# Squared-ReLU attention into a PReLU MLP: another order of the head, and bursts of three chunks, A@V and three chunks

## The chip, the cores and the metric

The kernel runs on one core of a Trainium2 chip. The metric is the device time of one execution, in microseconds (us). The core has a matrix engine (TensorE, PE in the profile, with its weight loads shown as PEld), a vector engine (VectorE, DVE), a scalar engine (ScalarE, ACT), GpSimd (POOL) and SyncE (SP). Here POOL does little but start the loads from memory, and SP starts the stores and the transposing transfers. Matrix products land in PSUM, which has 8 banks of 512 float32 per partition; only ACT and DVE bring them out again.

## The reference

```python
def _attn_ref(q, k, v):                       # 8 batches, 12 heads, 448 rows, 64 columns
    scale = 1.0 / np.sqrt(q.shape[-1])
    scores = scale * np.matmul(q, k.transpose(0, 1, 3, 2))
    attn = np.maximum(scores, 0.0) ** 2 / S
    return np.matmul(attn, v)

def _moe_ref(x, w_in, w_out, alpha):          # x: 3584 x 768, w_in: 768 x 2048, w_out: 2048 x 768
    h = x @ w_in
    g = np.maximum(h, 0.0) + alpha * np.minimum(h, 0.0)
    return g @ w_out
```

Between the two the heads are put side by side, so that x has one row of 12 * 64 values for each batch and row.

## The kernel before

**The units.** Four heads of one batch are a quad. A batch b has three, n = 3b to 3b + 2, so there are 24. The 448 rows of a head are cut into 7 sets of 64. A *chunk* (n, j) is the scores of the 64 keys of set j against all 448 queries, for the four heads of the quad. It goes through four lines:

- `score_mm` (L175): four matmuls on 64x64 parts of the array, into a pair of PSUM banks;
- `relu`: out of PSUM to bf16, 128x896, on ACT (L184) or on DVE (L186), as a letter A or D in the program says;
- `square`: times itself, on DVE (L194) or, for one chunk alone, on ACT (L192);
- `attnv(n)` ("A@V", L204): 28 matmuls, four for each of the quad's seven squared chunks in order, into a pair of banks. They give x transposed, which comes out scaled: for quad 0 in one ACT instruction of 128x896 (L212), for all others in two halves, one on ACT (L214) and one on DVE (L215).

For each batch F1 (`f1`, L238) makes 16 column blocks of h, called ff 0 to 15, each of 6 matmuls with km 0 to 5. km 0 and 1 read the first quad's x, 2 and 3 the second's, 4 and 5 the third's. `f1_out` brings each out by a ReLU of the negative on ACT (`neg`, L246) and one DVE instruction that forms g (L247), and then squares one waiting chunk, if there is one (`sq(1)`). For each pair of batches F2 (`f2`, L261) makes 7 x 2 tiles of the output with 16 matmuls each. ACT copies them out of PSUM (`osb`, L263) and SP stores them (L269).

**Turned rows.** q and k must be turned for the scores. Quads 0 to 5 are turned by the matrix engine (`turn_pe`: 28 transposes at L150, then copies out of PSUM on DVE at L153 or on ACT at L155). Quads from 6 on are turned by a transfer (`turn_dma`): DVE writes q and k into one tile in another order (`perm`, L161, two instructions), and SP starts a transposing transfer (L163). `prepare(n)` is `turn_dma(n)` and the loads of quad n + 2.

**What sets the order.** The order is written by hand: each engine gets its instructions in the order of the program text, and each waits in that order for what it needs. SP's transposes and stores and POOL's loads stand in their queues likewise. A PSUM bank is taken by `take_bank` (the one taken longest ago), a pair by `take_pair`; this too is settled in the order of the text, so a change of the order moves all later work to other banks. `hold` takes a bank and keeps it out of the choice until `take` is called for it. Tiles come from pools with fixed counts of buffers: 3 for the rows of q and of k, 7 for v, 2 for `perm`, 4 for the turned rows, 7 for relu results, 12 for squares, 4 for outputs. A tile waits until the one that had its buffer is done with.

**The head** is the program up to the first F2 tile: quads 0, 1 and 2 with little else to do beside them, then F1 of batch 0 with the chunks of quads 3 and 4 between its blocks. The four banks for ff 0 to 3 are kept early, km 0 to 3 of ff 0 and 1 run before A@V of quad 2, and km 0 to 3 of ff 2 and 3 behind it; then km 4 and 5 of all four.

**The body.** F1 of batch 1 follows, then for each batch two stretches. In the F1 stretch three chunks (`run(some(3))`) stand ahead of ff 6 and of ff 12. In the F2 stretch stand three bursts, one for each quad of the next batch; `burst(n)` is three chunks, `attnv(n)`, two chunks, and then the squares. Between two bursts there are two F2 tiles in even batches and three in odd ones. `some` deals out the chunks of quads 6 to 23 in order with the letters A, D, A. The last batch has no chunks left.

Of the kernel before, what the change touches and what calls it, by code (L numbers as in the profile page):

```python
# [12 lines left out]
ACTF = mybir.ActivationFunctionType  # L13
ALU = mybir.AluOpType

PP = 64
NJ = 7
# [3 lines left out]
def kernel(  # L21
# [10 lines left out]
    nc = tc.nc  # L32
    B, H, S, D = q.shape
# [3 lines left out]
    KM = d_model // 128  # L37
# [24 lines left out]
    psum = ps_pool.tile([128, 8, 512], F32)  # L62


    taken = [0] * 8
    clock = [0]

    def take(lo, n):
        clock[0] += 1
        for i in range(lo, lo + n):  # L70
            taken[i] = clock[0]

    def take_pair():
        lo = min((0, 2, 4, 6), key=lambda i: (max(taken[i], taken[i + 1]), i))
        take(lo, 2)
        return psum[:, lo:lo + 2]

    def hold():

        i = min(range(8), key=lambda i: (taken[i], i))  # L80
        taken[i] = 10**9
        return i

    def take_bank():
        i = min(range(8), key=lambda i: (taken[i], i))
        take(i, 1)
        return psum[:, i]
# [54 lines left out]
    def turn_pe(n, cuts=((0, NJ, "D"),), cuts_k=((0, NJ, "D"),)):  # L142
        t = T_pool.tile([128, 2, NJ, 128], BF16, tag="T", name="T")
        for i, name in enumerate("qk"):
            src = raw.pop((n, name))
            for lo, hi, eng in (cuts, cuts_k)[i]:
                ps = take_bank().bitcast(BF16)
                for j in range(lo, hi):
                    for s in range(2):
                        nc.tensor.transpose(ps[64 * s:64 * s + 64, 128 * j:128 * j + 128], src[:, s, j], ident)  # L150
                dst = t[:, i, lo:hi].rearrange("p j c -> p (j c)")
                if eng == "D":
                    nc.vector.tensor_copy(dst, ps[:, 128 * lo:128 * hi])  # L153
                else:
                    nc.scalar.copy(dst, ps[:, 128 * lo:128 * hi])  # L155
        T[n] = t

    def turn_dma(n):
        p = perm_pool.tile([128, 2, NJ, 2, D], BF16, tag="perm", name="perm")
        for i, name in enumerate("qk"):  # L160
            nc.vector.tensor_copy(p[:, i], raw.pop((n, name)).rearrange("p s j d -> p j s d"))  # L161
        t = T_pool.tile([128, 2, NJ, 128], BF16, tag="T", name="T")
        nc.sync.dma_start_transpose(out=t.rearrange("p a j c -> p (a j) c"),  # L163
                                    in_=p.rearrange("p a j s d -> p (a j s d)"))
        T[n] = t
# [20 lines left out]
            nc.vector.tensor_scalar(rl, ps[:, :, :S], 0.0, None, ALU.max)  # L186
        return rl

    def square(n, j, rl, eng="D"):
        a = at_pool.tile([128, 2, S], BF16, tag="at", name="at")  # L190
        if eng == "A":
            nc.scalar.activation(a, rl, ACTF.Square)  # L192
        else:
            nc.vector.tensor_tensor(a, rl, rl, ALU.mult)  # L194
        att[(n, j)] = a

    def attnv(n):
        ps = take_pair()
        vv = vraw.pop(n)
        for j in range(NJ):  # L200
            a = att.pop((n, j))
            for r in range(2):
                for s in range(2):
                    nc.tensor.matmul(ps[64 * s:64 * s + 64, r, :S],  # L204
                                     vv[64 * r:64 * r + 64, s, j, :],
                                     a[64 * r:64 * r + 64, s],
                                     start=(j == 0), stop=(j == NJ - 1))
        b, g = divmod(n, NG)
        if g == 0:
            xT[b] = xT_pool.tile([128, NG, 2, S], BF16, tag="xT", name="xT")  # L210
        if n == 0:
            nc.scalar.activation(xT[b][:, g], ps[:, :, :S], ACTF.Copy, scale=out_scale)  # L212
            return
        nc.scalar.activation(xT[b][:, g, 0], ps[:, 0, :S], ACTF.Copy, scale=out_scale)  # L214
        nc.vector.tensor_scalar(xT[b][:, g, 1], ps[:, 1, :S], out_scale, None, ALU.mult)  # L215

    late = []

    def sc(chunks):

        for n, j, eng in chunks:
            late.append((n, j, relu(score_mm(n, j), eng)))

    def sq(k=99):
        for g in late[:k]:
            square(*g)
        del late[:k]

    def run(chunks):
        sc(chunks)  # L230
        sq()


    gT = {}

    def f1_mm(ps, b, ff, ks):
        for km in ks:
            nc.tensor.matmul(ps, w_in_sb[:, km // 2, km % 2, bass.ts(ff, 128)],  # L238
                             xT[b][:, km // 2, km % 2, :],
                             start=(km == 0), stop=(km == KM - 1))  # L240

    def f1_out(ps, b, ff):
        if b // 2 not in gT:
            gT[b // 2] = g_pool.tile([128, KF, 2 * S], BF16, tag="g", name="gT")
        neg = neg_pool.tile([128, S], F32, tag="neg", name="neg")
        nc.scalar.activation(neg, ps, ACTF.Relu, scale=-1.0)  # L246
        nc.vector.scalar_tensor_tensor(gT[b // 2][:, ff, (b % 2) * S:(b % 2) * S + S],  # L247
                                       neg, beta_sb[:, ff:ff + 1], ps, ALU.mult, ALU.add)
        sq(1)
# [24 lines left out]
    def ch(n, lo, hi, p=pat):  # L274
        return [(n, j, p[j]) for j in range(lo, hi)]

    load_w_in(0)
    load_w_in(1)
    turn_pe(0, ((0, 4, "D"), (4, NJ, "D")), ((0, 2, "A"), (2, NJ, "D")))
    sc(ch(0, 0, 4))  # L280
    sq(3)
    load_qk(3)
# [15 lines left out]
    sc([(1, 4, "D"), (1, 5, "A"), (1, 6, "A")])  # L298
    sq(2)
    load_w_out(0)  # L300
    early = {}
    todo = []

    def some_early(count):
        for ff, km in todo[:count]:
            if ff not in early:
                early[ff] = hold()
            f1_mm(psum[:, early[ff], :S], 0, ff, (km,))
        del todo[:count]

    sc(ch(2, 0, 3, "AAA"))
    sq(3)
    attnv(1)
    load_qk(5)
    load_v(5)
    load_w_out(1)
    todo = [(ff, km) for ff in range(4) for km in range(4)]
    sc(ch(2, 3, 4, "AAAAAAA"))
    nc.vector.tensor_scalar(beta_sb, alpha_sb, -1.0, 1.0, ALU.mult, ALU.add)
    sq(2)  # L320
    sc(ch(2, 4, 7, "AAAAADA"))
    some_early(8)
    square(*late.pop(-2), "A")
    sq()
    attnv(2)
    some_early(8)
    for ff in range(4):
        f1_mm(psum[:, early[ff], :S], 0, ff, range(4, KM))
        f1_out(psum[:, early[ff], :S], 0, ff)
        take(early[ff], 1)  # L330


    def f1s(b, lo, hi):
        for ff in range(lo, hi):
            f1(b, ff)
# [6 lines left out]
    def prepare(n):  # L342
        if n < NQ:
            turn_dma(n)
        load(n + 2)

    turn_pe(3)
    load_qk(6)
    load_v(6)
    f1s(0, 4, 6)  # L350
    sc(ch(3, 0, 3))
    f1s(0, 6, 8)
    sc(ch(3, 3, 6))
    f1s(0, 8, 10)
    turn_pe(4)
# [27 lines left out]
    def some(k):  # L383
        lo = at_c[0]
        at_c[0] = min(lo + k, len(chunks))
        return [(n, j, e) for (n, j), e in zip(chunks[lo:at_c[0]], "ADA")]

    def burst(n):

        sc(some(3))  # L390
        attnv(n)
        sc(some(2))
        sq()

    early = []
    for ff in range(4):
        ps = take_bank()[:, :S]
# [4 lines left out]
    for ff in range(KF):  # L402
        if ff < 4:
            f1_mm(early[ff], 1, ff, range(4, KM))
            f1_out(early[ff], 1, ff)
        else:
            f1(1, ff)
        if ff in (1, 4, 7):
            turn_dma(6 + ff // 3)
        if ff == 11:  # L410
            load(9)
            load(10)
    f2(0, 3, 0)
    run(some(3))
    f2(0, 3, 1)
    f2(0, 0, 1)
    prepare(9)
    run(some(3))
    f2(0, 1, 1)
    run(some(3))  # L420
    f2(0, 2, 1)
    run(some(3))
    f2(0, 4, 0)
    burst(6)
    f2(0, 4, 1)
    f2(0, 5, 0)
    prepare(10)
    burst(7)
    f2(0, 5, 1)
    f2(0, 6, 0)  # L430
    burst(8)
    f2(0, 6, 1)

    for b in range(2, B):
        n0 = NG * (b + 1)
        last = b == B - 1
        sb = b // 2
        for ff in range(KF):
            if not last and ff in (6, 12):
                run(some(3))  # L440
            if not last and ff in (1, 9):
                prepare(n0 + 2 + ff // 8)
            f1(b, ff)
        if b % 2 == 0:
            units = [(sb, c, h) for c in range(3) for h in range(2)]
            at = {1: 0, 3: 1, 5: 2}
        else:
            units = [(sb, c, h) for c in range(3, 7) for h in range(2)]
            at = {1: 0, 4: 1, 7: 2}
        for i, u in enumerate(units):  # L450
            if i in at and not last:
                g = at[i]
                if g == 1:
                    prepare(n0 + 4)
                burst(n0 + g)
            if last and i == len(units) - 1:
                f2(*u, parts=((0, 256), (256, HALF)))
            else:
                f2(*u)
# [30 lines left out]
```

## Time and profile before

| What | Value |
|---|---|
| Median of three runs | 389.79 us (389.78 to 390.1) |
| The profiled execution | 389.79 us; its span, from the first to the last instruction, 388.0 us |
| PE busy | 378.4 us of the span, 98% |
| DVE, ACT, POOL busy | 266.2 us, 203.8 us, 63.3 us |
| Granted TensorE clock | 0.998 of full speed |

How to read the views. The *page* gives busy times for the whole span. The *table by stage* gives, for each stretch of the span, how long each engine was busy. The *timeline* lists instructions in order of time, like ones in a row put together: start, length, engine, line, operation, output and inputs, shapes, count, and in brackets how long the engine had been idle and what ended it. The *chain* is the work that ended last, followed back from the end: start, length, and what it was. In a row of like instructions each begins before the one ahead of it has ended, so the length of one is more than the step from start to start; both are used below and told apart.

### The profile page before, as it was taken

What the parts mean: (1) busy time and instruction counts of PE and PEld (TensorE: products, weight loads), DVE (VectorE), ACT (ScalarE), POOL (GpSimd) and SP (SyncE); (2) the same over time, 40 slices, a digit from 0 to 9 for tenths busy, and PEclk for the clock granted to TensorE, in tenths of its full rate; (3) what the DMA queues carried; (4) which work ended last, traced back from release to release, by engine and by line L of the source; (5) the groups of instructions that cost most, each with busy time, mean ns of one, the idle gap of its engine ahead of it and who ended that gap; (6) DMA issues with size and microseconds to landing.
All of it is one profiled execution on the core that took longest, in us unless ns stands there. A gap on an engine that the chain in (4) does not pass through costs nothing.

```text
span 388.0 us, 7917 instructions
## 1 busy us (share of the span) xinstructions
PE 378.4 (98%) x3228; PEld 210.6 (54%) x3228; DVE 266.2 (69%) x422; ACT 203.8 (53%) x329; POOL 63.3 (16%) x94
## 2 busy tenths in 40 slices
PE   7799999999999999999999999999999999999996
PEld 5444454555665456644555455654555545655564
DVE  4977965776868878789755897689754887626300
ACT  5977656445545665466444564546543475434311
POOL 7468211422022102022010220120000000000000
PEclk9999999999999999999999999999999999999999
DMA  9999999899593775787292872937024300120023
GB/s 180 188 203 204 204 214 209 133 173 180 119 151 75 119 127 78 134 131 112 54 170 57 138 114 47 169 56 143 24 62 100 78 0 23 42 61 2 13 70 82
DMA packets 71093, 43.06 MB, mean 111 GB/s; under 512 B 38160, under 2 KB 71056, under 8 KB 71056
## 3 DMA queue, kind: packets, MB, share of 16 engines
q0 software_dynamic: 26496, 22.35, 39.6%
q1 hardware_dynamic: 44128, 19.65, 23.6%
q10 hardware_dynamic: 432, 0.56, 0.4%
q8 instruction: 25, 0.41, 0.4%
q14 instruction: 12, 0.10, 0.1%
HBM read 45.62 MB, written 11.01 MB: 146 GB/s over the span
## 4 chain that ended last, share of the span: by engine, by line
PE 90%; DVE 5%; ACT 2%; DMA 1%; issue 1%; ACTq 0%
PE psum L261 38%; PE psum L238 35%; PE psum L204 8%; PE psum L175 8%; DVE at L194 2%; ACT rl L184 2%; DMA qfirst<-in_q_dram 1%; DVE gT L247 1%; PE psum L150 1%; DVE T L153 1%; DVE rl L186 1%; ACT neg L246 0%; ACT osb L263 0%; DVE qraw L133 0%; ACTq L269 0%
## 5 line engine op out<-in xcount | busy, mean ns | idle before, releaser
L261 PE MATMUL psum<-w_out_sb,gT 128*128 128x384 bf16 (+2 forms) x912 | 151.1, 323 | 0.1
L238 PE MATMUL psum<-xT,w_in_sb 128*128 128x448 bf16 x768 | 149.5, 353 | 0.4 <-ACT rl L184 0.4
L261 PEld LDWEIGHTS <-gT 128*128 128x128 bf16 x912 | 86.7, 98 | 63.1 <-issue 8.6
L238 PEld LDWEIGHTS <-w_in_sb 128*128 128x128 bf16 x768 | 73.7, 98 | 72.3 <-issue 5.5
L246 ACT ACTIVATE neg<-psum 128x448 f32<-128x448 f32 x128 | 69.2, 546 | 66.2 <-PE psum L238 62.4
L247 DVE SCALAR_TENSOR_TENSOR gT<-neg,beta_sb,psum 128x448 bf16<-128x448 f32 x128 | 83.1, 676 | 29.5 <-ACT neg L246 29.5
L184 ACT ACTIVATE rl<-psum 128x896 bf16<-128x896 f32 x115 | 99.7, 934 | 0.5 <-PE psum L175 0.5
L194 DVE TENSOR_TENSOR at<-rl 128x896 bf16<-128x896 bf16 x167 | 93.7, 617 | 2.1 <-ACT rl L184 2.0
L186 DVE TENSOR_SCALAR rl<-psum 128x896 bf16<-128x896 f32 x53 | 57.5, 1086 | 40.3 <-PE psum L175 40.2
L263 ACT COPY osb<-psum 128x384 f32<-128x384 f32 (+2 forms) x57 | 27.0, 474 | 105.8 <-PE psum L261 98.9
L175 PE MATMUL psum<-T 64*64 64x448 bf16 x672 | 45.9, 356 | 2.4 <-ACT rl L184 0.9
L97 POOL DMA_DIRECT2D qraw<-in_q_dram x23 | 16.5, 717 | 179.1 <-DVE perm L161 167.6
L204 PE MATMUL psum<-at,vraw 64*64 64x448 bf16 x672 | 37.2, 351 | 0.6 <-ACT rl L184 0.2
L204 PEld LDWEIGHTS <-vraw 64*64 64x64 bf16 x672 | 23.9, 106 | 11.4 <-issue 3.2
L175 PEld LDWEIGHTS <-T 64*64 64x64 bf16 x672 | 18.0, 105 | 22.1 <-issue 15.6
L215 DVE TENSOR_SCALAR xT<-psum 128x448 bf16<-128x448 f32 x23 | 14.4, 625 | 16.0 <-PE psum L204 11.6
L97 POOL DMA_DIRECT2D kraw<-in_k_dram x23 | 16.5, 719 | 7.8 <-PE psum L175 4.8
L104 POOL DMA_DIRECT2D vraw<-in_v_dram x24 | 17.3, 722 | 2.0 <-DMA w_in_sb<-in_moe_w_in_dram 0.9
L214 ACT ACTIVATE xT<-psum 128x448 bf16<-128x448 f32 x23 | 12.7, 553 | 4.3 <-PE psum L204 4.3
L161 DVE COPY perm<-qraw 128x896 bf16<-128x896 bf16 x18 | 11.0, 611 | 4.9 <-DMA T<-perm 2.6
L114 POOL DMA_DIRECT2D w_in_sb<-in_moe_w_in_dram x16 | 10.0, 628 | 7.5 <-DMA kraw<-in_k_dram 2.5
L161 DVE COPY perm<-kraw 128x896 bf16<-128x896 bf16 x18 | 10.9, 608 | 0.0
(21 smaller groups left out, 35.3 us busy)
## 6 DMA issues: line engine op xcount, KB each, us to landing
out_dram<-osb SPq DMA_DIRECT2D x110, 96.0 KB, 2.2
vraw<-in_v_dram POOLq DMA_DIRECT2D x24, 224.0 KB, 7.4
qraw<-in_q_dram POOLq DMA_DIRECT2D x23, 224.0 KB, 4.7
kraw<-in_k_dram POOLq DMA_DIRECT2D x23, 224.0 KB, 6.7
w_in_sb<-in_moe_w_in_dram POOLq DMA_DIRECT2D x16, 192.0 KB, 8.2
w_out_sb<-in_moe_w_out_dram POOLq DMA_DIRECT2D x2, 1536.0 KB, 18.5
qfirst<-in_q_dram SPq DMA_DIRECT2D x1, 448.0 KB, 4.3
kfirst<-in_k_dram ACTq DMA_DIRECT2D x1, 448.0 KB, 4.6
```

The costliest lines, as they stand in the source:

```text
L97: nc.gpsimd.dma_start(out=t.rearrange("p m j d -> p m (j d)"), in_=flat[:, 2 * g:2 * g + 2])
L161: nc.vector.tensor_copy(p[:, i], raw.pop((n, name)).rearrange("p s j d -> p j s d"))
L175: nc.tensor.matmul(ps[64 * c:64 * c + 64, r, :S], t[64 * r:64 * r + 64, 1, j, 64 * c:64 * c + 64], t[64 * r:64 * r + 64, 0, :, 64 * c:64 * ...
L184: nc.scalar.activation(rl, ps[:, :, :S], ACTF.Relu)
L186: nc.vector.tensor_scalar(rl, ps[:, :, :S], 0.0, None, ALU.max)
L194: nc.vector.tensor_tensor(a, rl, rl, ALU.mult)
L204: nc.tensor.matmul(ps[64 * s:64 * s + 64, r, :S], vv[64 * r:64 * r + 64, s, j, :], a[64 * r:64 * r + 64, s], start=(j == 0), stop=(j == NJ ...
L238: nc.tensor.matmul(ps, w_in_sb[:, km // 2, km % 2, bass.ts(ff, 128)], xT[b][:, km // 2, km % 2, :], start=(km == 0), stop=(km == KM - 1))
L246: nc.scalar.activation(neg, ps, ACTF.Relu, scale=-1.0)
L247: nc.vector.scalar_tensor_tensor(gT[b // 2][:, ff, (b % 2) * S:(b % 2) * S + S], neg, beta_sb[:, ff:ff + 1], ps, ALU.mult, ALU.add)
L261: nc.tensor.matmul(ps, gT[sb][:, ff, bass.ts(c, 128)], w_out_sb[:, hf, ff, lo:hi], start=(ff == 0), stop=(ff == KF - 1))
L263: nc.scalar.copy(o[:, lo:hi], ps)
```

## The change

Eight things change.

1. In `turn_pe(0)` the copy of the first two sets of k's columns moves from ACT to DVE.
2. `attnv(1)` gets its result out in one ACT instruction of 128x896, as `attnv(0)` does, in place of two halves on ACT and DVE.
3. Ahead of `attnv(1)` stand two chunks of quad 2 and two squares, in place of three and three; the third chunk comes behind it. Three squares then follow where two did.
4. The squared chunk (2, 5) moves from ACT to DVE; `square` loses its ACT form.
5. Ahead of `attnv(2)` km 0 to 3 of ff 0 and 1 still run, but ff 2 and 3 no longer begin behind it; km 4 and 5 of ff 0 follow it at once. `hold` goes. ff 2 runs whole ahead of `turn_pe(3)`, and the blocks around the chunks of quad 3 are cut at 3, 5 and 8 in place of 4, 6 and 8. The new condition for the tile of g makes it at the same place as before.
6. A burst is three chunks, A@V, three chunks. For this the run of three chunks behind `f2(0, 2, 1)` goes, and in each F1 stretch the two runs ahead of ff 6 and ff 12 become one ahead of ff 8.
7. `turn_dma` of quads 6, 7 and 8 stands behind ff 1, 5 and 9 of batch 1 in place of 1, 4 and 7, and the loads of quads 9 and 10 behind ff 13 in place of 11.
8. `prepare(9)` moves behind `f2(0, 4, 0)`, ahead of the first burst, and `prepare(10)` ahead of the third. In the later batches it stands at ff 8 and ahead of the first and third bursts, in place of ff 1, ff 9 and ahead of the second burst.

```diff
-    if eng == "A":
-        nc.scalar.activation(a, rl, ACTF.Square)
-    else:
-        nc.vector.tensor_tensor(a, rl, rl, ALU.mult)
+    nc.vector.tensor_tensor(a, rl, rl, ALU.mult)
...
-    if n == 0:
+    if n < 2:
         nc.scalar.activation(xT[b][:, g], ps[:, :, :S], ACTF.Copy, scale=out_scale)
         return
...
-    if b // 2 not in gT:
+    if b % 2 == 0 and ff == 0:
...
-turn_pe(0, ((0, 4, "D"), (4, NJ, "D")), ((0, 2, "A"), (2, NJ, "D")))
+turn_pe(0, ((0, 4, "D"), (4, NJ, "D")), ((0, 2, "D"), (2, NJ, "D")))
...
-sc(ch(2, 0, 3, "AAA"))
-sq(3)
+sc(ch(2, 0, 2, "AA"))
+sq(2)
 attnv(1)
 ...
-todo = [(ff, km) for ff in range(4) for km in range(4)]
-sc(ch(2, 3, 4, "AAAAAAA"))
+sc(ch(2, 2, 4, "AAAAAAA"))
 nc.vector.tensor_scalar(beta_sb, alpha_sb, -1.0, 1.0, ALU.mult, ALU.add)
-sq(2)
+sq(3)
 sc(ch(2, 4, 7, "AAAAADA"))
-some_early(8)
-square(*late.pop(-2), "A")
 sq()
+early = []
+for ff in range(2):
+    ps = take_bank()[:, :S]
+    f1_mm(ps, 0, ff, range(4))
+    early.append(ps)
 attnv(2)
-some_early(8)
-for ff in range(4):
-    f1_mm(psum[:, early[ff], :S], 0, ff, range(4, KM))
-    f1_out(psum[:, early[ff], :S], 0, ff)
-    take(early[ff], 1)
+for ff in range(2):
+    f1_mm(early[ff], 0, ff, range(4, KM))
+    f1_out(early[ff], 0, ff)
...
+f1s(0, 2, 3)
 turn_pe(3)
 load_qk(6)
 load_v(6)
-f1s(0, 4, 6)
+f1s(0, 3, 5)
 sc(ch(3, 0, 3))
-f1s(0, 6, 8)
+f1s(0, 5, 8)
...
 def burst(n):
     sc(some(3))
     attnv(n)
-    sc(some(2))
+    sc(some(3))
     sq()
...
-    if ff in (1, 4, 7):
-        turn_dma(6 + ff // 3)
-    if ff == 11:
+    if ff in (1, 5, 9):
+        turn_dma(6 + ff // 4)
+    if ff == 13:
         load(9)
         load(10)
...
-prepare(9)
 run(some(3))
 f2(0, 1, 1)
 run(some(3))
 f2(0, 2, 1)
-run(some(3))
 f2(0, 4, 0)
+prepare(9)
 burst(6)
 f2(0, 4, 1)
 f2(0, 5, 0)
-prepare(10)
 burst(7)
 f2(0, 5, 1)
 f2(0, 6, 0)
+prepare(10)
 burst(8)
...
-        if not last and ff in (6, 12):
+        if not last and ff == 8:
             run(some(3))
-        if not last and ff in (1, 9):
-            prepare(n0 + 2 + ff // 8)
+            prepare(n0 + 2)
...
-            if g == 1:
-                prepare(n0 + 4)
+            if g != 1:
+                prepare(n0 + 3 + g // 2)
             burst(n0 + g)
```

More of the change, by code (lines that the diff above doesn't have):

```diff
@@ L76, in take_pair @@
         return psum[:, lo:lo + 2]
[L78 to L82, printed above, removed]
     def take_bank():
@@ L187, in relu, with square @@
         return rl
-    def square(n, j, rl, eng="D"):
+    def square(n, j, rl):
         a = at_pool.tile([128, 2, S], BF16, tag="at", name="at")
-        if eng == "A":
-            nc.scalar.activation(a, rl, ACTF.Square)
-        else:
-            nc.vector.tensor_tensor(a, rl, rl, ALU.mult)
+        nc.vector.tensor_tensor(a, rl, rl, ALU.mult)
         att[(n, j)] = a
@@ L300 @@
     load_w_out(0)
[L301 to L309, printed above, removed]
-    sc(ch(2, 0, 3, "AAA"))
-    sq(3)
+    sc(ch(2, 0, 2, "AA"))
+    sq(2)
     attnv(1)
```

## The prediction

> **What bounds the kernel now.** I read the page first, then the table by stage, the chain, and the timeline where the first two point. The page's row of PE:
>
> ```profile
> PE 378.4 (98%) x3228; PEld 210.6 (54%) x3228; DVE 266.2 (69%) x422; ACT 203.8 (53%) x329; POOL 63.3 (16%) x94
> ```
>
> The table by stage (start and end, length, then each engine's busy us):
>
> ```profile
> 5.00:25.00 20.00, 15.87 (x262) 8.63 (x262) 18.60 (x34) 18.24 (x25) 11.84 (x19) 1.00 1.26 189
> 25.00:65.00 40.00, 39.50 (x399) 20.34 (x398) 30.01 (x50) 26.10 (x41) 15.02 (x21) 1.00 1.28 208
> 65.00:120.00 55.00, 55.00 (x451) 30.99 (x449) 39.99 (x64) 28.52 (x47) 10.72 (x15) 1.00 0.94 153
> 120.00:345.00 225.00, 225.00 (x1845) 124.31 (x1843) 166.69 (x262) 116.49 (x191) 21.43 (x30) 1.00 0.49 88
> ```
>
> PE is idle for 4.1 us of the first stage, with DVE (18.6 of 20) and ACT (18.2) both nearly full, and never from 65 to 345 us. So the change can gain or lose in two places: in the head, through what ACT and DVE finish last, and in the body, through PE's own steps or a wait that is not there yet.
>
> The end of the head on PE, ACT and DVE:
>
> ```profile
> 21.76 1.67 PE L238 MATMUL psum<-xT,w_in_sb 128*128 128x448 bf16 x8 [0.43 <-ACT rl L184]
> 23.37 1.52 PE L204 MATMUL psum<-at,vraw 64*64 64x448 bf16 x28
> 24.82 3.20 PE L238 MATMUL psum<-xT,w_in_sb 128*128 128x448 bf16 x16
> ```
> ```profile
> 20.18 0.73 ACT L214 ACTIVATE xT<-psum 128x448 bf16<-128x448 f32 x1
> 20.60 2.73 ACT L184 ACTIVATE rl<-psum 128x896 bf16<-128x896 f32 x3
> 22.99 1.17 ACT L192 ACTIVATE at<-rl 128x896 bf16<-128x896 bf16 x1
> 24.92 0.55 ACT L214 ACTIVATE xT<-psum 128x448 bf16<-128x448 f32 x1 [0.76 <-PE psum L204]
> ```
> ```profile
> 21.70 1.08 DVE L186 TENSOR_SCALAR rl<-psum 128x896 bf16<-128x896 f32 x1
> 22.70 1.69 DVE L194 TENSOR_TENSOR at<-rl 128x896 bf16<-128x896 bf16 x3
> 24.96 0.62 DVE L215 TENSOR_SCALAR xT<-psum 128x448 bf16<-128x448 f32 x1 [0.58 <-PE psum L204]
> ```
>
> ACT works without a gap from 7.40 to 24.16 us. PE goes from A@V of quad 2 straight into 16 matmuls of F1; the first eight (ff 2 and 3) don't need that A@V, and cover the two instructions that bring its result out.
>
> The chain through one F1 stretch, and a burst's A@V result with the F2 tile behind it:
>
> ```profile
> 120.83 6.81 PE psum L238 x36
> 127.64 0.69 PE psum L175 x12
> 128.33 6.92 PE psum L238 x36
> 135.24 0.69 PE psum L175 x12
> 135.94 4.65 PE psum L238 x24
> ```
> ```profile
> 345.40 18.16 PE psum L238 x96
> ```
> ```profile
> 109.95 0.54 ACT L214 ACTIVATE xT<-psum 128x448 bf16<-128x448 f32 x1
> 110.09 0.62 DVE L215 TENSOR_SCALAR xT<-psum 128x448 bf16<-128x448 f32 x1 [0.54 <-ACT rl L184]
> 110.29 0.66 PE L261 MATMUL psum<-w_out_sb,gT 128*128 128x384 bf16 x3
> ```
>
> **The change, part by part.** The profiled execution took 389.79 us, which is the median too; 1.79 lie outside its span of 388.0 and are kept. Steps from start to start in an unbroken row: ACT's relu or whole x copy 0.80, DVE's square 0.53, DVE's relu 1.00, a chunk on PE 0.19, an F1 matmul 0.19. A release reaches the next engine in 0.03 to 0.05.
>
> *k's copy to DVE (1).* DVE's copy of q's last 384 columns runs 6.57 to 6.92. The 256 columns of k, estimated at 0.28 from the copies of 512 and 384 columns (0.43, 0.35), then end at 7.12, and the first chunk starts at 7.17, not 6.97. On ACT they hid beside DVE. From here ACT and DVE pace the head, so all of it moves by 0.20.
>
> *A@V of quad 1 (2, 3).* Its last quarter waits for the square of chunk (1, 6), on DVE from 18.89, now 19.09 to 19.70; PE ends at 20.14 (before 19.94). ACT has one relu less to do meanwhile: its relu of (2, 1) starts at 18.78, so it is free at 19.58 and idles to 20.19. The whole copy then takes it to 20.99, where a half took 0.42. Relus of (2, 2), (2, 3), (2, 4), (2, 6) start at 20.99, 21.78, 22.58, 23.38.
>
> *Square (2, 5) to DVE (4).* DVE runs dry at 20.8, gets the first of these relus at 21.90, and does square (2, 2) from 21.93, the relu of (2, 5) from 22.47, then four squares from 23.47 to 25.69; the last ended at 24.38 before. ACT's square, gone, was not behind anything. The last quarter of A@V of quad 2 starts at 25.74, before at 24.53: **+1.21**. The eight F1 matmuls ahead of it run at 22.8 and cover none of this.
>
> *No ff 2 and 3 behind it (5).* A@V ends at 26.13, ACT's half takes 0.55 from 26.17, and km 4 starts at 26.77: 1.03 after the last quarter's start, where F1 followed after 0.29: **+0.74**. Behind that PE had no wait up to 34.3 us; the blocks cut at 3, 5, 8 put one more square ahead of the second group of quad 3, so DVE's full stretch from 37.84 to 47.35, which ends in a wait of 0.18 at the first F2 tile, is one square (0.53) shorter: **-0.18**. Head together **+1.8**. Bounds: 1.2 if only the first term stands, 2.5 if one further ACT step (0.8) falls in.
>
> Two rules of the Trainium skill pull apart here. "ScalarE: Activation LUTs", rules for kernel authors, gives relu and mul to VectorE as up to about three times faster in bf16; the square rows, 1.17 on ACT and 0.62 on DVE, fit its direction. By it the moved square would be worth ACT's 0.80, and the time 388.8 in place of the sum below. "TensorEngine Tiling (Array Packing)", PSUM bottleneck, wants both engines to empty PSUM, and so speaks against part 2; the rows, 0.42 for ACT's half against 0.80 for the whole, agree. By it alone that would cost 0.38, and the time would be 390.0. I go by the order of waits above, in which neither price stands alone.
>
> *Fewer excursions (6).* The stretch above lasts 6.81 + 0.69 + 6.92 + 0.69 + 4.65 = 19.76; 96 matmuls alone take 18.16, six chunks 1.13. So leaving for three chunks and coming back costs (19.76 - 18.16 - 1.13) / 2 = 0.23. One goes ahead of the bursts and one in each of five batches; the chunks themselves move into the bursts at their 0.19. Six times 0.23: **-1.4** (1.2 to 1.5).
>
> *The tile behind a burst (6, and the banks that follow).* By the order of takes, the F2 tile behind a burst had the third chunk's bank, free after ACT's second relu. After the change it takes the low bank of A@V's own pair, in all 17 bursts that have six chunks. That bank is freed by ACT's half, which in bursts of the trace ends 2.66 to 2.73 after the burst's first matmul (here 109.95 + 0.54 - 107.83). The tile starts at 2.46, with a sixth chunk 2.65; with 0.05 for the release it can start at 2.71 to 2.78. I take 0.07 each, **+1.2**. Bounds: 0, if the records are 0.07 off, and 0.12 each, 2.0.
>
> *Transfers and queues (7, 8).* Costed at nothing, by these covers. POOL's loads (three issues of 0.7 a quad) wait for the `perm` copies that free their buffers, not for their place (167.6 us of waits), and follow those. DVE's two `perm` copies take 1.1: between bursts DVE then has 2.0 + 0.5 + 3.2 + 1.1 = 6.8 of 8.0 us to do. At ff 8 they stand with a relu and three squares, so g of ff 8 comes about 3.7 late, while 8 banks let PE run on for more than 5. SP holds stores behind a transpose (1.3 to 3.5 as a rule); four output buffers at 2.6 each cover that. The tightest is quad n0 + 2: `perm` ends 5.1 after the run's first matmul, the transfer lands 6.9 later (median; 9.0 beside late loads), by 12 to 14.2, and its first chunk, the last of the first burst, stands at 15.0. With the cover gone, each us late costs 1 us in five batches. Nothing is to be gained here, as PE is never idle there.
>
> Sum: 389.8 + 1.8 - 1.4 + 1.2 = **391.4**.
>
> **The rivals.**
>
> - *A, the bursts stay free.* The tile's wait is hidden in the step from chunk to F2, which in these bursts is 0.36 where elsewhere it is 0.29. It decides below 2.65 for the end of ACT's half. The margin is small; against it, all bursts show 2.66 or more. 389.8 + 1.8 - 1.4 = 390.2: not slower.
> - *B, ACT alone paces the head.* If the squares of (1, 5) and (1, 6) come 0.6 earlier, ACT doesn't idle and the missing square helps: the last quarter slips by 0.08 alone, the lost cover (0.74) stays. 390.4. Against it: DVE's row is unbroken from 14.68.
> - *C, F1's first stretch swallows the head's loss.* DVE's full stretch (37.8 to 47.4) is in the chain; if it were anchored before 34 us, PE's delay would not reach its end: 389.6. Against it, DVE was idle for 1.5 us at 36.3, behind chunks that PE had reached without a wait.
> - *D, the run at ff 8 is too much.* Relu, squares and `perm` together hold g back until PE lacks a bank: 0.5 in five batches, 394. From 5 us of delay on; I count 3.7.
> - *E, turned rows come late.* At the longest landing of the trace, 17.0, five waits of 7 us: 426; at 11, 396. The 17 stands where three transposes lay within 9 us, which happens once.
>
> **How the numbers follow.** About 0.2% (0.8 us) is what a measurement can tell from no change. Chances: my forecast 0.61, A 0.14, B 0.08, C 0.08, D 0.05, E 0.04. Forecast, D and E are slower (0.70), and of A and B 0.07; the same are 0.14 of A and B and 0.03 of C; faster 0.05 of C, with a little more for A and B together (389.0): 0.06 in all. The forecast's own range joins its bounds: 389.8 + 1.2 - 1.5 + 0.5 = 390.0 to 389.8 + 2.5 - 1.2 + 2.0 = 393.1. A and B lie in it; down to 389.7 it takes half of C. D and E are left out.
>
> **What would show it.** Right: the last quarter of A@V of quad 2 near 25.7, and PE idle for some 0.6 behind it until ACT's half ends; ACT idle near 19.6 ahead of the whole x copy; three chunks once in each F1 stretch; the tile behind each burst 2.7 after the burst's start, on the heels of ACT's half. Wrong: F1 back at 25 us (B), the tile at 2.65 with a gap behind ACT (A), a shift that is there at 34 us and gone at 47 (C), or PE idle at F1 behind ff 8 or at the last chunk of a first burst (D, E).

## The result, and the profile after

The changed kernel takes 391.43 us (median, 391.24 to 391.54) against 389.78 for the kernel before in the same call: slower, by a ratio of 1.0040 with a 95% interval of 1.0023 to 1.0058. The profiled execution's span is 389.7 us, 1.7 more than before.

The page's row of PE and the table by stage of the changed kernel answer to those shown of before (start and end, length, then each engine's busy us):

```profile
PE 378.6 (97%) x3228; PEld 216.5 (56%) x3228; DVE 263.8 (68%) x418; ACT 207.5 (53%) x332; POOL 63.3 (16%) x94
```
```profile
5.00:25.00 20.00, 15.10 (x248) 8.42 (x249) 17.81 (x33) 17.44 (x22) 11.63 (x19) 1.00 1.26 190
25.00:65.00 40.00, 39.04 (x400) 20.29 (x396) 30.04 (x50) 25.48 (x40) 15.21 (x21) 1.00 1.28 208
65.00:120.00 55.00, 54.90 (x469) 31.36 (x462) 38.30 (x61) 28.64 (x48) 10.72 (x15) 1.00 0.79 130
120.00:345.00 225.00, 224.77 (x1845) 128.80 (x1845) 166.67 (x261) 121.49 (x197) 21.43 (x30) 1.00 0.56 93
```

PE does the same 3228 matmuls. In the first stage it, DVE and ACT are all less busy than before: the head has more waiting, not more work. From 65 to 345 us PE is again busy to within 0.3 us.

The end of the head, from the timelines of PE, ACT and DVE of the changed kernel:

```profile
21.37 0.38 PE L169 MATMUL psum<-T 64*64 64x448 bf16 x4 [0.45 <-ACT xT L203]
22.17 0.38 PE L169 MATMUL psum<-T 64*64 64x448 bf16 x4 [0.42 <-ACT rl L178]
22.98 1.67 PE L229 MATMUL psum<-xT,w_in_sb 128*128 128x448 bf16 x8 [0.43 <-ACT rl L178]
24.59 1.77 PE L195 MATMUL psum<-at,vraw 64*64 64x448 bf16 x28
26.98 1.49 PE L229 MATMUL psum<-xT,w_in_sb 128*128 128x448 bf16 x7 [0.62 <-ACT xT L205]
```
```profile
20.40 0.92 ACT L203 ACTIVATE xT<-psum 128x896 bf16<-128x896 f32 x1 [0.33 <-PE psum L195]
21.21 3.34 ACT L178 ACTIVATE rl<-psum 128x896 bf16<-128x896 f32 x4
26.39 0.54 ACT L205 ACTIVATE xT<-psum 128x448 bf16<-128x448 f32 x1 [1.83 <-PE psum L195]
```
```profile
22.16 0.63 DVE L185 TENSOR_TENSOR at<-rl 128x896 bf16<-128x896 bf16 x1 [1.09 <-ACT rl L178]
22.70 1.08 DVE L180 TENSOR_SCALAR rl<-psum 128x896 bf16<-128x896 f32 x1
23.70 2.22 DVE L185 TENSOR_TENSOR at<-rl 128x896 bf16<-128x896 bf16 x4
26.43 0.62 DVE L206 TENSOR_SCALAR xT<-psum 128x448 bf16<-128x448 f32 x1 [0.51 <-PE psum L195]
```

ACT idles ahead of the whole copy of A@V of quad 1, DVE then has nothing to do for 1.09 us until the first relu behind that copy, and its last square ends at 25.92. A@V of quad 2 takes 1.77 in place of 1.52, as its last quarter waits for that square, and F1 begins only behind ACT's half of its result.

The chain through one F1 stretch, and a burst's A@V result with the F2 tile behind it:

```profile
122.73 9.08 PE psum L229 x48
131.81 0.69 PE psum L169 x12
132.50 9.19 PE psum L229 x48
```
```profile
119.37 0.54 ACT L205 ACTIVATE xT<-psum 128x448 bf16<-128x448 f32 x1
119.51 0.62 DVE L206 TENSOR_SCALAR xT<-psum 128x448 bf16<-128x448 f32 x1 [0.54 <-ACT rl L178]
119.81 0.91 ACT L178 ACTIVATE rl<-psum 128x896 bf16<-128x896 f32 x1
119.97 0.81 PE L252 MATMUL psum<-w_out_sb,gT 128*128 128x384 bf16 x4
```

The stretch is 18.96 long, 0.80 less than before: three chunks at 0.19 and one excursion at 0.23. The burst began at 117.25, so the F2 tile starts 2.72 behind it, 0.06 behind the end of ACT's half. In all 17 bursts it stands 2.71 to 2.82 behind. In the bursts of before, which have one chunk less, it stood 2.46 to 2.51 behind (2.27 in the last, with one chunk behind A@V). The step from the matmul ahead of the tile to the tile's first, 0.28 in all 17 bursts of before, is now 0.34 to 0.41, which is 1.37 longer in all 17 together.

Where the matrix engine is later than before, at five places of the two traces:

| Place | Before | After | Later by |
|---|---|---|---|
| First chunk | 6.97 | 7.38 | 0.41 |
| Last quarter of A@V of quad 2 | 24.53 | 25.97 | 1.44 |
| F1 behind it | 24.82 | 26.98 | 2.16 |
| First F2 tile | 47.39 | 49.36 | 1.97 |
| F1 of the last batch | 345.24 | 346.94 | 1.70 |

So the head loses 2.0 and the body gives back 0.3.

### The profile page after: what moved, and what is told of

The parts are those of the page before. It is cut to its first block, busy times and chain, and to the rows that moved or that the text cites. A ratio compares the mean times of both kernels' runs of the same rounds, so it can differ in the third digit from the quotient of the medians.

```text
span 389.7 us, 7952 instructions
## 1 busy us (share of the span) xinstructions
PE 378.6 (97%) x3228; PEld 216.5 (56%) x3228; DVE 263.8 (68%) x418; ACT 207.5 (53%) x332; POOL 63.3 (16%) x94
## 4 chain that ended last, share of the span: by engine, by line
PE 87%; ACT 5%; DVE 3%; DMA 2%; issue 2%; ACTq 0%
PE psum L252 37%; PE psum L229 36%; PE psum L169 7%; PE psum L195 6%; ACT rl L178 4%; DVE at L185 2%; DMA qfirst<-in_q_dram 1%; DVE T L147 1%; PE psum L144 1%; ACT xT L205 1%; DVE rl L180 1%; DMA out_dram<-osb 1%; DVE gT L238 0%; ACT osb L254 0%; DVE qraw L127 0%
## 5 line engine op out<-in xcount | busy, mean ns | idle before, releaser
L252 PEld LDWEIGHTS <-gT 128*128 128x128 bf16 x912 | 87.6, 98 | 61.5 <-issue 6.7
L238 DVE SCALAR_TENSOR_TENSOR gT<-neg,beta_sb,psum 128x448 bf16<-128x448 f32 x128 | 84.3, 677 | 41.3 <-ACT neg L237 40.9
L178 ACT ACTIVATE rl<-psum 128x896 bf16<-128x896 f32 x120 | 102.9, 928 | 1.4 <-PE psum L169 1.4
L180 DVE TENSOR_SCALAR rl<-psum 128x896 bf16<-128x896 f32 x48 | 52.1, 1086 | 37.1 <-PE psum L169 37.1
L169 PE MATMUL psum<-T 64*64 64x448 bf16 x672 | 44.8, 355 | 3.8 <-DVE T L147 1.4
L169 PEld LDWEIGHTS <-T 64*64 64x64 bf16 x672 | 20.9, 105 | 21.6 <-issue 14.6
L195 PEld LDWEIGHTS <-vraw 64*64 64x64 bf16 x672 | 24.8, 106 | 10.9 <-issue 3.4
```

The lines of the kernel that those rows point to most:

```text
L169: nc.tensor.matmul(ps[64 * c:64 * c + 64, r, :S], t[64 * r:64 * r + 64, 1, j, 64 * c:64 * c + 64], t[64 * r:64 * r + 64, 0, :, 64 * c:64 * ...
L178: nc.scalar.activation(rl, ps[:, :, :S], ACTF.Relu)
L195: nc.tensor.matmul(ps[64 * s:64 * s + 64, r, :S], vv[64 * r:64 * r + 64, s, j, :], a[64 * r:64 * r + 64, s], start=(j == 0), stop=(j == NJ ...
L252: nc.tensor.matmul(ps, gT[sb][:, ff, bass.ts(c, 128)], w_out_sb[:, hf, ff, lo:hi], start=(ff == 0), stop=(ff == KF - 1))
```

## The experiments

Times are medians (one execution for `no4_again`). Beside them the kernel before took 390.08 with `head_only`, `body_only`, `whole_after` and `whole_before`, 389.78 with `no2`, `no3`, `no5` and `split`, 390.18 with `no4`, `no34` and `no23`, and 389.72 with `no4_again`.

**The head alone, and the rest alone.** `head_only` joins the changed program up to F1 of batch 1 to the body as it was; `body_only` does the reverse.

```diff
head_only:   parts 1 to 5 as changed, 6 to 8 as before
body_only:   parts 1 to 5 as before, 6 to 8 as changed
```

> Parts 1 to 5 alone (the head as changed, up to F1 of batch 0), with bursts, runs, transfers and their places as before. My theory, from the two traces: the head delays the matrix engine by 2.0 us and nothing gives it back, so 391.8, with A@V of quad 5 some 2 us later than before and the last batch's F1 as late as that. Rival C (F1's first stretch, full on DVE, swallows the delay): 389.8 to 390.2, the delay seen at 27 us and gone at 50.

> Parts 6 to 8 alone, with the head as before. My theory: six excursions less (-1.4) and 17 waits of the F2 tile for ACT's half of A@V (+1.2) nearly cancel, so 389.5, and the tile behind each burst starts 2.71 to 2.82 after the burst's first matmul. Rival A (no such wait): 388.4. Rival that the body lost too: over 390.5.

`head_only` took 391.94, a ratio of 1.0053 (1.0035 to 1.0071): the head holds the whole loss. Counted from the first chunk, the last quarter of A@V of quad 2 stands at 18.60 and the first F2 tile at 42.00, as in the changed kernel (18.59 and 41.98), against 17.56 and 40.42 before. So nothing of it is swallowed up to there, and from the first chunk to the end of the span it is 382.58 against 381.05. Rival C falls. `body_only` took 389.70 against 390.08, a ratio of 0.9989 (0.9981 to 0.9998): ahead of both kernels by a little, and far from the 388.4 of a body without the wait.

**The tile behind a burst.** ACT brings out all of A@V's result in the bursts, once in the changed kernel and once in the kernel before. DVE has less to do.

```diff
whole_after:
-        if n < 2:
+        if n < 2 or 6 <= n < 23:
whole_before:
-        if n == 0:
+        if n == 0 or 6 <= n < 23:
```

> The changed kernel, with A@V of quads 6 to 22 brought out in one ACT instruction (0.80 a step) in place of an ACT half (0.42) and a DVE half. My theory (the F2 tile behind a burst waits for ACT to free the low bank of A@V's pair): each of 17 tiles starts 0.38 later, 391.4 + 6.4 = 397.8, with the tile 3.1 after the burst's start. Rival P (the 0.43 between the sixth chunk and the tile is the matrix engine's own step, not a wait): 391.4, the tile still at 2.72.

> The same edit in the kernel before, where the tile behind a burst has the third chunk's bank. My theory: nobody waits there for A@V's result, so 389.8 to 390.1 and the tile still at 2.46 to 2.51. Rival Q (ACT is so full in the bursts that any 0.38 more on it reaches the matrix engine, whatever bank the tile has): some 395 to 396.

398.73 for the one, 390.12 for the other (ratio to before 1.0002, 0.9992 to 1.0011). Timeline rows of the changed kernel with the whole copy, and the row of its waits for the 17 bursts (in total, times, longest):

```profile
120.36 0.92 ACT L203 ACTIVATE xT<-psum 128x896 bf16<-128x896 f32 x1
```
```profile
121.33 0.97 PE L252 MATMUL psum<-w_out_sb,gT 128*128 128x384 bf16 x5 [0.44 <-ACT xT L203]
```
```profile
PE psum L252 <- ACT xT L203: 7.5, 17, 0.4
```

The copy ends 0.92 after its start and no longer 0.54, the tile goes to 3.15 to 3.21 after the burst's start, and 17 times 0.43 is the 7.3 by which the kernel is longer. I had put it at 6.4, from ACT's step instead of the instruction's length. In the kernel before, the same longer copy leaves the tile where it was in all 17 bursts. So the wait is there, it comes with the bank, and ACT's load in the bursts is not what matters.

**What an excursion costs.** The run of three chunks becomes three runs of one.

```diff
split:
-            if not last and ff == 8:
-                run(some(3))
-                prepare(n0 + 2)
+            if not last and ff in (8, 10, 12):
+                run([some(1)[0][:2] + ("ADA"[ff // 2 - 4],)])
+            if not last and ff == 8:
+                prepare(n0 + 2)
```

> The changed kernel with the run of three chunks ahead of ff 8 split into three runs of one, ahead of ff 8, 10 and 12: ten excursions more, no work more, with the letters and transfers as they were. My theory: each costs the matrix engine 0.23: +2.3, 393.8. Rival (what an excursion costs is the wait for its banks, which three chunks at once need and one doesn't): 391.4 or less.

393.64, or 2.21 more than the changed kernel for ten excursions more: 0.22 each. In the traces each of the five F1 stretches is 19.42 long in place of 18.96, for two more: 0.23 each. Its chain shows single chunks that cost 0.31 where the step between chunks is 0.19, and 2.38 for twelve F1 matmuls (2.27 at 0.189 each):

```profile
131.66 0.31 PE psum L169 x4
131.98 2.38 PE psum L229 x12
134.35 0.31 PE psum L169 x4
134.67 2.38 PE psum L229 x12
137.04 0.31 PE psum L169 x4
137.36 4.65 PE psum L229 x24
```

**The parts of the head, one by one.** Each of these is the changed kernel with some parts undone.

```diff
no2:
-        if n < 2:
+        if n < 1:
no3:
-    sc(ch(2, 0, 2, "AA"))
-    sq(2)
+    sc(ch(2, 0, 3, "AAA"))
+    sq(3)
     attnv(1)
...
-    sc(ch(2, 2, 4, "AAAAAAA"))
+    sc(ch(2, 3, 4, "AAAAAAA"))
...
-    sq(3)
+    sq(2)
     sc(ch(2, 4, 7, "AAAAADA"))
no4:
     sc(ch(2, 4, 7, "AAAAADA"))
+    square(*late.pop(-2), "A")
     sq()
no5:       hold, some_early and the cuts at 4, 6 and 8 as before
no23:      the edits of no2 and no3
no34:      the edits of no3 and no4
```

> The changed kernel with part 2 undone: A@V of quad 1 comes out in halves on ACT and DVE. My theory: ACT is done with it 0.38 earlier, all later relus of quad 2 with it, DVE has over 1 us to spare there, so the last square, the last quarter of A@V of quad 2 and the end move by -0.4: 391.0. If ACT did not matter here (DVE alone paces the head): 391.4 or, with DVE's half added, 391.9.

> The changed kernel with part 3 undone: three chunks of quad 2 ahead of A@V of quad 1. My theory: ACT no longer idles 0.4 to 0.6 ahead of the whole copy, its later relus come 0.6 earlier, and DVE, which no longer runs dry, ends its last square about 1 us earlier; the last quarter of A@V then moves by 0.8, and the end too: 390.6. Rival (the idle time is harmless, as DVE's squares pace the head anyway): 391.3 to 391.4.

> The changed kernel with part 5 undone: km 0 to 3 of ff 2 and 3 run behind A@V of quad 2. My theory: they cover the two instructions that bring its result out, so F1 follows 0.29 after the last quarter's start and not 1.01: -0.72, and the one square more in DVE's later stretch gives back 0.19: 390.9. Rival B (that cover is worth nothing, since the next stretch is paced by DVE): 391.4.

> The changed kernel with part 4 alone undone: the square of chunk (2, 5) on ACT again. My theory now (DVE's row of squares paces the end of the head, and ACT gets to this square only behind its last relu, at about 24.4): DVE's last square ends 0.53 earlier, but ACT's ends at 25.6, so the last quarter of A@V of quad 2 gains 0.15 to 0.2 only, counted from the first chunk; 391.2 to 391.3. If the square's place were what the head lost: 390.9.

> Parts 3 and 4 undone. My theory now: with part 3 undone ACT runs without a gap and gets to the square in time, so here the square on ACT takes DVE's last square 0.27 further forward than part 3 alone did: 17.67 from the first chunk to the last quarter of A@V of quad 2 (17.94 with part 3 undone alone, 18.59 in the changed kernel, 17.56 in the kernel before); 390.3. If part 4 is worth the same wherever part 3 stands: 17.8, 390.4.

> Parts 2 and 3 undone, the square of (2, 5) still on DVE. My theory now: DVE has no time to spare once it takes the half of A@V of quad 1 (0.53) too, so this is worse than part 3 undone alone: 18.2 from the first chunk to the last quarter of A@V of quad 2, in place of 17.94; 390.8. If ACT's shorter copy were what counts (my forecast's view of part 2): 17.6, 390.2.

> The kernel of no4 once more, for an execution whose clock is not halved in the head, as it was in the one profiled. My theory as there: from the first chunk to the last quarter of A@V of quad 2 18.4 to 18.45, in place of 18.59 in the changed kernel. If the square's place were what the head lost: 18.1.

The first chunk starts earlier or later from execution to execution (see the last section), so the places in the head are counted from it. The times come from several rounds of runs, in which the kernel before took 389.72 to 390.18, so the parts are compared by the places. "Eight F1 matmuls" is the start of the eight (km 0 to 3 of ff 0 and 1) that stand ahead of A@V of quad 2; "last square" is the end of the last square that this A@V reads.

| Kernel | Time | Eight F1 matmuls | Last square | Last quarter of A@V of quad 2 | F1 behind it | First F2 tile |
|---|---|---|---|---|---|---|
| before | 389.78 | 14.79 | 17.41 | 17.56 | 17.85 | 40.42 |
| after | 391.43 | 15.60 | 18.54 | 18.59 | 19.60 | 41.98 |
| no2 | 391.24 | 15.22 | 18.49 | 18.54 | 19.55 | 41.94 |
| no3 | 390.58 | 15.18 | 17.67 | 17.94 | 18.93 | 41.32 |
| no23 | 390.82 | 14.80 | 17.96 | 18.02 | 19.03 | 41.41 |
| no34 | 390.72 | 15.17 | 17.56 | 17.93 | 18.92 | 41.31 |
| no4_again | 391.21 | 15.61 | 18.01 | 18.37 | 19.36 | 41.75 |
| no5 | 390.73 | 15.61 | 18.55 | 18.60 | 18.92 | 41.50 |

The table shows two limits. PE reaches the last quarter 2.76 or 2.77 behind the start of the eight matmuls, and these wait for a bank that ACT frees with a relu. The last square must be done too, 0.05 or 0.06 ahead. In each row the last quarter starts at the later of the two: by the bank in before, `no3`, `no34` and `no4_again`, by the square in the other four. For the bank, parts 2 and 3 are worth 0.4 each: 15.60 with both, 15.22 and 15.18 with one undone, 14.80 with both undone. That is 0.81 of the 1.03 by which the changed kernel's last quarter is late; its last square comes 0.22 behind that.

- `no5` does as expected: the last quarter stays, F1 follows it after 0.32 in place of 1.01, and 0.2 of that is given back by the first F2 tile.
- `no3` gives 0.65 at the last quarter. It was put at 0.8. It is the one part of the three about A@V of quad 1 and the squares that is worth much by itself.
- `no2` was a miss: 0.05, not 0.4. ACT is indeed done earlier and the bank comes 0.38 earlier, but DVE's row with the half in it runs unbroken to the last square.

Timeline of DVE in `no2`, from the half to the last square:

```profile
20.10 0.62 DVE L206 TENSOR_SCALAR xT<-psum 128x448 bf16<-128x448 f32 x1 [0.51 <-PE psum L195]
20.64 0.16 DVE L299 TENSOR_SCALAR beta_sb<-alpha_sb 128x16 f32<-128x16 f32 x1
20.71 1.69 DVE L185 TENSOR_TENSOR at<-rl 128x896 bf16<-128x896 bf16 x3
22.32 1.08 DVE L180 TENSOR_SCALAR rl<-psum 128x896 bf16<-128x896 f32 x1
23.32 2.22 DVE L185 TENSOR_TENSOR at<-rl 128x896 bf16<-128x896 bf16 x4
```

No row behind the first has a wait. DVE's wait of 0.51 ahead of the half and the half itself (0.53 to the next start) take the place of the 1.09 that it idled, and the last square ends 0.05 earlier only.

- `no4`: its profiled execution had the clock of TensorE halved from 22.81 to 26.22 us, so it says nothing on the head; its median is 391.25. `no4_again` is the same kernel, in an execution without that: the last quarter comes 0.22 earlier, a little more than the 0.14 to 0.19 expected, and the time is 391.21 (one execution). A@V of quad 2 then runs through without waiting for a square, so what is left is the late bank:

```profile
24.54 1.52 PE L198 MATMUL psum<-at,vraw 64*64 64x448 bf16 x28
```

- `no34` was a miss: with part 3 undone, the square's place is worth nothing (17.93 against 17.94).

The timeline of PE in `no34` shows why:

```profile
21.66 0.38 PE L169 MATMUL psum<-T 64*64 64x448 bf16 x4 [0.43 <-ACT xT L206]
22.47 1.67 PE L232 MATMUL psum<-xT,w_in_sb 128*128 128x448 bf16 x8 [0.43 <-ACT rl L178]
24.07 1.52 PE L198 MATMUL psum<-at,vraw 64*64 64x448 bf16 x28
```

A@V runs through in 1.52, so no square is late. What is late is its start: the eight F1 matmuls ahead of it wait for a bank that ACT frees, behind the whole copy of part 2. With part 2 undone too but not part 4 (`no23`), those matmuls start as early as before, and A@V's last quarter waits for a square again (idle for 0.15), as DVE has the half and the square: 18.02, the right way from 17.94 but less far than the 18.2 expected. Only with 2, 3 and 4 all undone, as in the head of before, is it 17.56 (that head lacks parts 1 and 5 too; part 5 does not move this place, as `no5` shows, and the places are counted from the first chunk). So the head has two limits within a microsecond, DVE's squares and the bank from ACT, and undoing one part shows only the way to the other.

## Why the prediction was right

The time was put at 391.4 and came out at 391.43. By its terms:

- **k's copy to DVE, 0.20.** The first chunk is 0.41 later. In `before` and `whole_before`, where ACT has this copy, it comes 1.20 and 1.19 after the first transpose; in `head_only`, `no2`, `no3` and `no5`, where DVE has it, 1.39 or 1.40. That is the 0.20; the copy itself takes 0.28, as estimated. The other 0.2 goes with the clock (last section), not with the change.
- **A@V of quad 1, and the square, +1.21.** With the 0.20 above in it, it measures 0.20 + 1.03. The chain was as put, idle ACT, late relus, DVE dry and then six instructions in a row, and each is in the rows above: DVE waited 1.09 where 1.1 was put. What the prediction left out is the second limit. It has the eight F1 matmuls ahead of A@V at 22.8 and says that they cover none of the delay; but they are themselves 0.81 late, behind the same late relus, so without any late square the last quarter would still have slipped by 0.81. So the longer copy does not count in the sum in the way that was put: part 2 undone alone gives 0.05, part 3 0.65, part 4 0.22, and the whole 1.03 shows only when all three are undone.
- **The lost cover, +0.74, and -0.18 given back.** Measured 0.72 and -0.19, and by `no5` 0.68 and 0.2.
- **Six excursions, -1.4.** 0.23 by the chain, 0.22 by `split`.
- **The tile behind a burst, +1.2.** The body as a whole gives 0.28 back up to the last batch's F1, so with -1.4 for the excursions the waits cost 1.1 by difference, where 1.2 was put. Read directly, the steps ahead of the 17 tiles are 1.37 longer; 0.2 of that comes back in the tile's next step, 0.162 in place of 0.173. The tiles are at 2.71 to 2.82, where 2.71 to 2.78 was put; `whole_after` and `whole_before` show the cause. The forecast's range takes 0.5 as the least for this term, though its bound was put at 0, which would make the low end 389.5; the result does not turn on that.
- **Transfers and queues, nothing.** A row of busy time can't show this, since waits as short as those of the tiles are hidden in it. But all five F1 stretches of the changed kernel are 18.96 long, which 96 matmuls (18.16), three chunks (0.57) and one excursion (0.23) fill, so nothing holds up PE behind ff 8. And the tile behind the first burst of each of the five batches stands at 2.72, as behind the others, so its last chunk did not wait for quad n0 + 2. The five transfers of that quad land 1.1 to 6.3 before the quad's first chunk starts; the 1.1 is that of quad 17. Their covers were not taken away by a run.

The head comes to 0.20 + 1.03 + 0.72 - 0.19 = 1.76 where 1.8 was put. That sum holds for the profiled pair only after 0.2 for the clock is taken off: the two spans differ by 1.65, and 1.76 + 0.2 - 0.28 is 1.68. The prediction had no term for the clock. By the terms measured alone, 1.76 - 0.28, the time would be 391.3. That the median came within 0.03 of what was put is closer than these terms are known, and in part luck; how much of the 0.2 is in the median of four executions is not known.

The rivals: A falls with `whole_after` and `body_only`. B falls in that ACT did idle ahead of the whole copy and the last quarter slipped by 1.03, not by 0.08; in `no4_again` and `no34` the square on ACT is no burden that anything waits for. B was near in one thing, as a limit set by ACT stands 0.22 behind that of DVE. C falls with `head_only`, and D and E with the stretches and first bursts above.

Of the two rules, that of "ScalarE: Activation LUTs", which gives mul to VectorE, points the wrong way here: undoing part 4 brought F1 0.24 forward, since DVE's squares and not ACT ended the head (with part 3 undone it made no difference). The page gives its factor of three for operations with one source; the square's rows, 1.17 and 0.62, give 1.9. That of "TensorEngine Tiling (Array Packing)", both engines on PSUM, is not shown by part 2 undone alone (0.05), because DVE had no time left for its half. With 3 and 4 undone as well, part 2 is worth 0.37 (17.93 in `no34`, 17.56 in before), and 0.38 was the price put by that rule.

## What to carry to other kernels

When two engines feed a third without a gap, ask which of them ends last at each place before moving an instruction from one to the other; undoing parts one at a time can undercount them, as each only uncovers the next limit. When fewer and larger groups save switches, look at who gets which bank next: here the 1.4 from six switches less was eaten, all but 0.3, by 17 short waits, because a matmul came to stand behind the result that had been written last. And matmuls that don't need a result belong right behind the ones that make it: eight of them were worth 0.7.

## What the runs showed of the hardware that was not expected

**The clock of TensorE at the start.** The kernel runs 36 matmuls to warm up, from 1.36 us on in both profiles. Full clock is recorded from 4.47 us in the profile of before and from 6.82 us in that of after; over the fourteen profiles it begins between 4.11 and 7.15. The first transposes show it (PE, after and then before, 14 transposes each of q and of k):

```profile
5.75 0.96 PE L144 MATMUL psum<-ident,qraw 128*64 128x128 bf16 x14 [0.37 <-DVE qraw L127]
6.50 0.71 PE L144 MATMUL psum<-ident,kraw 128*64 128x128 bf16 x14
```
```profile
5.77 0.58 PE L150 MATMUL psum<-ident,qraw 128*64 128x128 bf16 x14 [0.76 <-DVE qraw L133]
6.19 0.78 PE L150 MATMUL psum<-ident,kraw 128*64 128x128 bf16 x14
```

With k's copy on DVE, the first chunk comes 1.39 to 1.40 after the first transpose in the eight profiles where full clock began at 4.11 to 5.93, 1.47 in `split`, where it began at 5.95, and 1.62 to 1.63 where it began at 6.82 or 7.15. "TensorE: Matmul & The Clock Gate", part 1, says that the window which decides is free-running, so that the point moves from run to run; these profiles agree. A difference of 0.2 between two profiles of this kernel can be this alone.

**The clock can fall again in the head.** In the profile of `no4` it was halved for 3.41 us from 22.81. The table by stage, ahead of the fall and in it (the eighth number is the clock):

```profile
19.40:22.81 3.41, 1.96 (x29) 0.85 (x24) 2.32 (x6) 3.08 (x5) 2.17 (x4) 1.00 1.24 204
22.81:26.22 3.41, 3.41 (x16) 1.26 (x19) 2.33 (x4) 2.33 (x3) 2.01 (x4) 0.50 1.26 203
```

PE was busy for 1.96 of the 3.41 us before it. A second execution of the same kernel had like gaps (busy for 2.09 of the same 3.41 us) and no fall, so such a thin stretch of work on PE does not always bring it. From the first chunk, F1 behind A@V of quad 2 came 1.64 later in the one than in the other. Four more executions on record have as low a mean clock, 0.995 or 0.996, and are 1.3 to 2.0 us longer than the median of their kernel: two of the kernel before, one each of `head_only` and `no3`. So it is not particular to the kernel of `no4`, though no trace shows where their clock fell. That the phase of the window decides is a guess; no run tests it.
